# Weight decoding over two queued parts, later global exponentials, and a dense piece moved behind the turns of P

## The chip, the cores and the metric

The kernel runs on one core of one Trainium2 chip. The metric is the device time of one execution in microseconds (us), lower is better. TensorE multiplies matrices into PSUM; VectorE, ScalarE (ACT) and GpSimd (POOL) do elementwise work, each in the order of its own instruction queue; SyncE (SP) issues the DMAs. All of them meet only through semaphores, so a wait on one engine holds whatever stands behind it on that engine.

## The reference

The program computes a local attention with global tokens, then a dense feed-forward layer, then a mixture of experts.

```python
s_g = scale * np.matmul(q_g, k_all.transpose(0, 1, 3, 2))
out_g = np.matmul(sm(s_g), v_all)                    # 32 global queries see all keys
mask = np.abs(pos[:, None] - pos[None, :]) <= 32
s_l = np.concatenate([s_lg, np.where(mask, s_ll, -1e9)], axis=-1)
out_l = np.matmul(sm(s_l), np.concatenate([v_g, v_l], axis=2))
...
h = x @ w_in                                         # 2176 x 512 by 512 x 2048
x = (np.maximum(h, 0) + alpha * np.minimum(h, 0)) @ w_out
...
out[mask_e] = np.maximum(x[mask_e] @ w1[e], 0) @ w2[e]   # 8 experts, assigned greedily
```

There are 4 batches of 8 heads with 512 local and 32 global tokens and a head size of 64. The weights of the first dense layer arrive as float64, as pairs of 32-bit words, and are turned into fp32 on the chip ("decoded").

## The kernel before

The attention runs over 8 groups of four heads (index p), each in 4 steps of 128 queries (index j), so over 32 steps n = 4p + j, with two more to drain. Dense work is woven into it. It is software-pipelined by hand: `attention()` writes out the order of the instructions of TensorE, VectorE and ACT, and that order is kept.

One step n works on three steps' data at once. `norm` (L400) divides the probabilities of step n - 1 by their sums on VectorE. `scores` (L369) multiplies queries and keys of step n on TensorE (L388); four times VectorE adds the mask and takes the maximum (L394) and ACT takes the exponential with its sum (L396); GpSimd adds a small number to the sums (L398). Then `later` holds small VectorE work left over from the step before, among it the copy of the global attention output from PSUM (L472) and the global normalisation `gnorm`. `dense.close` finishes a dense row block: VectorE, ACT and GpSimd make its high and low halves. `wide_part` does the global queries: in a group's second step (j = 1) `gscores`, two matmuls with two VectorE maxima (L438) and one exponential on ACT (L442); in the fourth (j = 3) `gtrans`, which turns the global probabilities by TensorE (L461) in two parts; in the first and third `gpv`, their product with V (L470). `pv` (L421) multiplies the turned probabilities of step n - 2 with V, and `ptrans` (L410) turns those of step n - 1, "the turns of P".

From step BEG = 12 on, `dense.products` adds one piece of six matmuls per step of the first dense chunk, written out right behind the scores. A row block takes two pieces; its ReLU on ACT (L545) opens the next step (`dense.turn`). After the attention `dense.rest` goes on with that chunk, and the later chunks follow, on TensorE in an order written by hand.

`bank` gives PSUM buffers. The pool with the tag "y" has two buffers, which are taken in turn: a step takes one for the output of `pv` and then one for its global work. So the second part of the turn in the fourth step (`gt1`) gets the buffer of the third step's `gpv`, which L472 empties in the fourth step's `later`, behind the four masks of that step. SOLO is 8.

The first halves of the two dense weights are decoded in 16 parts during the attention. `decoding` (L77) is a generator: a DMA load (L79), one magnitude on ACT (L83), four VectorE instructions (L85, L88, L90, L92), and then a conversion on ACT and a subtraction on GpSimd (L72, L73). It yields "A" or "V" for the engine that comes next. `queue` holds two parts; `fill(kind, n)` drives up to n stages of that kind, and before the change only those of the queue's head. There are three load buffers.

SyncE's and GpSimd's orders are not fixed by hand in this stretch.

Of the kernel before, what the change touches and what calls it, by code (L numbers as in the profile page):

```python
# [14 lines left out]
AF = mybir.ActivationFunctionType  # L15
OP = mybir.AluOpType
# [9 lines left out]
def tile_attention_moe_moe(ctx: ExitStack, tc: tile.TileContext, qkw, vw,  # L26
                           w_in, w_out, gate, w1, w2, out):
    nc = tc.nc
    V, A, P, T = nc.vector, nc.scalar, nc.gpsimd, nc.tensor
# [282 lines left out]
    with ExitStack() as at:  # L312
# [11 lines left out]
        SOLO = (S // (4 * WIN)) * (H // 4)  # L324
        BEG = SOLO + 4

        def bank(shape, name):
            pool, tag = pY, "y"
            if name == "s" and wide[0]:
                pool, tag = pS, "s"  # L330
            elif name == "s":
                pool, tag = ((pS, "s"), (pS, "s"), (pH, "h1"), (pH, "h1"))[turn[0] % 4]
                turn[0] += 1
            elif name in ("t", "gs0", "gt0"):
                pool, tag = pX, "x"
            return pool.tile(shape, F32, name=name, tag=tag)
# [4 lines left out]
        G = [dict() for _ in range(NU // 2)]  # L341
# [29 lines left out]
        def scores(p, j):  # L371
            d = G[p]
            if j == 0:
                b, hp = units[2 * p]
                if hp == 0:
                    XB[b] = gx.tile([128, KD, ST], F32, name="xb", bufs=2)
                d["x"] = XB[b][:, hp:hp + 2]
            d["pr", j] = pp.tile([128, 4, KW], F32, name="pr")
            d["sm", j] = pp.tile([128, 4], F32, name="sm")
            d["mx", j] = pp.tile([128, 4], F32, name="mx")  # L380
            s = [bank([128, 2, KW], "s") for _ in range(2)]
            for ii in range(0, 4, 2):
                for e in range(2):
                    i = 4 * j + ii + e
                    for a in range(2):
                        u = 2 * p + a
                        for h, r in heads():
                            T.matmul(s[e][lane(2 * a + h, i), ii // 2], queries(u, i)[r], U[u]["k"][r, kpos(i):kpos(i) + KW],  # L388
                                     start=True, stop=True)
            for ii in range(4):  # L390
                i = 4 * j + ii
                m = mask[:, 0 if i == 0 else 2 if i == NQ - 1 else 1]
                sc = pp.tile([128, KW], F32, name="sc", bufs=4)
                V.tensor_tensor_reduce(out=sc, in0=s[ii % 2][:, ii // 2], in1=m, scale=-D ** -0.5, scalar=BIG,  # L394
                                       op0=OP.add, op1=OP.min, accum_out=d["mx", j][:, ii:ii + 1])
                A.activation(out=d["pr", j][:, ii], in_=sc, func=AF.Exp, bias=d["mx", j][:, ii:ii + 1], scale=-1.0,  # L396
                             accum_out=d["sm", j][:, ii:ii + 1])
            P.tensor_scalar(d["sm", j], d["sm", j], 1e-9, None, op0=OP.add)  # L398

        def norm(p, j):  # L400
            sm = G[p]["sm", j]
            V.reciprocal(sm, sm)
            pr = G[p]["pr", j]
            V.tensor_tensor(pr, pr, sm.unsqueeze(2).to_broadcast([128, 4, KW]), op=OP.mult)  # L404

        def ptrans(p, j):
            d = G[p]
            t = bank([128, 4, 128], "t")
            for ii in range(4):
                T.transpose(t[:, ii], d["pr", j][:, ii], ident)  # L410
            d["t", j] = tp.tile([128, 4, 128], F32, name="pt")
            A.copy(d["t", j], t)
# [14 lines left out]
        def gscores(p, part):  # L427
            d = G[p]
            if part == 0:
                d["s"] = (gp.tile([128, NG], F32, name="gsc"), gp.tile([128, 4], F32, name="gmx", bufs=2))  # L430
            sc, mx = d["s"]
            lo, hi = (0, S) if part == 0 else (S, NG)
            s = bank([128, hi - lo], f"gs{part}")
            for i in range(2):
                k = U[2 * p + i]["k"]
                x = k[:, WIN:2 * WIN] if part else k[:, 2 * WIN:KL - WIN].rearrange("p (m c) -> p m c", c=3 * WIN)[:, :, :2 * WIN]
                T.matmul(s[64 * i:64 * i + 64], U[2 * p + i]["g"], x, start=True, stop=True)
            V.tensor_tensor_reduce(out=sc[:, lo:hi], in0=s, in1=gzero.to_broadcast([128, hi - lo]), scale=-D ** -0.5,  # L438
                                   scalar=mx[:, 0:1] if part else BIG, op0=OP.add, op1=OP.min,
                                   accum_out=mx[:, part:part + 1])  # L440
            if part:
                A.activation(out=sc, in_=sc, func=AF.Exp, bias=mx[:, 1:2], scale=-1.0, accum_out=mx[:, 2:3])  # L442
                P.tensor_scalar(mx[:, 2:3], mx[:, 2:3], 1e-9, None, op0=OP.add)
                later.append(lambda: gnorm(p))

        def gnorm(p):
            sc, mx = G[p]["s"]
            V.reciprocal(mx[:, 3:4], mx[:, 2:3])
            own = gpat[:, 2 * WIN:KL - WIN].rearrange("p (m c) -> p m c", c=3 * WIN)[:, :, :2 * WIN]
            V.tensor_scalar(own, sc[:, :S].rearrange("p (m c) -> p m c", c=2 * WIN), mx[:, 3:4], None, op0=OP.mult)  # L450
            V.tensor_scalar(gpat[:, 4 * WIN:5 * WIN], sc[:, S:], mx[:, 3:4], None, op0=OP.mult)
# [32 lines left out]
        later, at_out = [], [None]  # L484

        def wide_part(n):
            p, j = divmod(n, STEPS)
            last = n == STEPS * NU // 2 + 1
            if j == 1 and not last:
                gscores(p, 0)  # L490
                gscores(p, 1)
            if j == 3:
                gtrans(p, 0)
                gtrans(p, 1)
            if p and (j == 0 or j == 2 or last):
                gpv(p - 1, 1 if last else j // 2)

        def attention():
            N = STEPS * NU // 2
            for n in range(N + 2):  # L500
                p, j = divmod(n, STEPS)
                if n < N and p and 2 * p + 2 < NU:
                    (load_qk, load_v)[j // 2](2 * p + 2 + j % 2)
                if n == SOLO - 1:
                    nc.sync.dma_start(out=ag, in_=gate)
                wide[0] = n >= SOLO
                dense.turn(n)
                if 1 <= n <= N:
                    norm(*divmod(n - 1, STEPS))
                if n < N:  # L510
                    scores(p, j)
                while later:
                    later.pop()()
                dense.close(n)
                fill("V", 2)
                o = None
                if n >= 2:
                    o = bank([128, 2, QS], "o")
                    for _ in range((2, 0, 2, 2)[j] if n < BEG else 0):
                        T.matmul(o[:, 0], ident, ident, start=True, stop=True)  # L520
                dense.products(n)
                wide_part(n)
                fill("V", 2 if n >= SOLO and n % 3 == 0 else 1 if n < SOLO else 0)
                if n >= 2:
                    v, j2 = divmod(n - 2, STEPS)
                    pv(v, j2, o)
                if p and j == 3:
                    gout(p - 1)
                if 1 <= n <= N:
                    ptrans(*divmod(n - 1, STEPS))  # L530
                if n > 2:
                    fill("A", 2)
                yield 0
            for f in later:
                f()
            gout(NU // 2 - 1)

        class dense:
            ps, ys, g, at, over = None, [], None, 0, []
# [66 lines left out]
        queue = []  # L606

        def fill(kind, n):
            if not queue:
                return  # L610
            st, at = queue[0]
            while n and at == kind:
                try:
                    at = next(st)
                    n -= 1
                except StopIteration:
                    queue.pop(0)
                    if ahead_:
                        queue.append(ahead_.pop(0))
                        queue[-1][1] = next(queue[-1][0])  # L620
                    if not queue:
                        return
                    st, at = queue[0]
            queue[0][1] = at

        ahead_ = [[win_steps(dc, 0, i), None] for i in range(2 * KD)] + [[wout_steps(dc, 0, i), None] for i in range(KH)]

# [45 lines left out]
    with tc.tile_pool(name="dc2", bufs=1, side="right") as dc, tc.tile_pool(name="pW", bufs=2, space=PSUM) as pW, \  # L673
# [4 lines left out]
        n = 0  # L678
# [20 lines left out]
    with ExitStack() as mo:  # L699
# [713 lines left out]
        for k in range(E):  # L1413
            n = 0.0
# [101 lines left out]
```

## Time and profile before

| | us |
|---|---|
| median of 3 runs (805.73 to 808.45) | 806.33 |
| profiled execution | 808.91 |
| its span on the core | 807.1 |
| TensorE matmul busy (share of the span) | 778.6 (96%) |
| TensorE weight load | 726.1 (90%) |
| VectorE | 451.8 (56%) |
| ACT | 392.4 (49%) |
| GpSimd | 368.1 (46%) |

Busy time of TensorE is modelled, so a high share is not yet a full engine: single waits must be looked for in its timeline. The shares are means over stages with different limits. The span is the profiled one; the median comes from runs without a profile.

### The profile page before, as it was taken

How to read it: one execution, taken by the hardware profiler on the slowest of the kernel's cores; microseconds unless marked ns; L12 is line 12 of the kernel's file. 1: busy time of each engine (PE TensorE's matmuls, PEld its weight loads, DVE VectorE, ACT ScalarE, POOL GpSimd, SP SyncE). 2: the span in 40 equal slices, each digit the busy share in tenths (PEclk: the TensorE clock that was granted, in tenths of full speed). 3: DMA queues.
4: the chain of work that ended last, by engine and by line, in shares of the span. 5: the costliest groups of instructions: out<-in, count | busy, mean ns of one | idle time of the engine just before them, and what ended most of it. 6: DMA issues, size and time to landing. Idle time of an engine off the chain costs nothing.

```text
span 807.1 us, 20873 instructions
## 1 busy us (share of the span) xinstructions
PE 778.6 (96%) x8290; PEld 726.1 (90%) x8290; DVE 451.8 (56%) x1555; ACT 392.4 (49%) x983; POOL 368.1 (46%) x348
## 2 busy tenths in 40 slices
PE   7899899999999999999999999999999999999996
PEld 4777678999999989999999999999899999999994
DVE  5899899265455621433433467776776777651210
ACT  5787788344544443333333425342564554454430
POOL 2243333054443552100000838473798988698611
PEclk9999999999999999999999999999999999999999
DMA  8988783632343112013221236243467656467510
GB/s 342 400 302 292 271 329 128 211 111 95 109 134 108 56 36 79 28 56 95 74 62 51 84 110 228 79 143 94 130 214 209 189 183 196 153 190 207 193 46 28
DMA packets 53850, 121.98 MB, mean 151 GB/s; under 512 B 4600, under 2 KB 26040, under 8 KB 51705
## 3 DMA queue, kind: packets, MB, share of 16 engines
q1 hardware_dynamic: 50825, 111.73, 42.0%
q0 software_dynamic: 2928, 8.92, 3.0%
q8 instruction: 65, 1.06, 0.5%
q14 instruction: 32, 0.26, 0.1%
HBM read 102.80 MB, written 17.83 MB: 149 GB/s over the span
## 4 chain that ended last, share of the span: by engine, by line
PE 72%; DVE 10%; DMA 6%; issue 4%; POOL 4%; ACT 3%; SPq 0%; POOLq 0%; DVEq 0%; ACTq 0%
PE h L200 21%; PE h L1272 10%; PE y L239 9%; PE h L1116 8%; PE h L1136 8%; POOL m L73 2%; DMA raw<-in_moe_w_dram 2%; DVE sc L394 2%; PE o L421 2%; DMA raw<-in_moe_w_in_dram 2%; DVE pr L404 2%; PE h L1349 2%; PE lp L282 2%; PE s L388 1%; PE t L410 1%
## 5 line engine op out<-in xcount | busy, mean ns | idle before, releaser
L73 POOL TENSOR_TENSOR m<-raw,m 128x1024 fp32r<-128x1024 f32 x64 | 152.1, 2399 | 18.5 <-ACT m L72 15.9
L200 PE MATMUL h<-xh,win 128*128 128x272 f32 x704 | 138.6, 291 | 1.4 <-ACT xd L245 1.4
L73 POOL TENSOR_TENSOR gr<-gb,gr 128x272 fp32r<-128x272 f32 x64 | 48.1, 791 | 149.3 <-ACT gr L72 148.9
L200 PEld LDWEIGHTS h<-xh,win 128*128 128x128 f32 x704 | 111.9, 188 | 4.0 <-issue 2.2
L1116 PE MATMUL h<-xsh,m 128*128 128x272 f32 x512 | 103.3, 294 | 0.0
L200 PE MATMUL h<-xl,win 128*128 128x272 f32 x352 | 101.3, 288 | 0.0
L1272 PE MATMUL h<-gr,wout 128*128 128x272 f32 x672 | 95.1, 294 | 0.0
L1136 PE MATMUL h<-hh,m 128*128 128x272 f32 x448 | 92.7, 298 | 0.0
L1272 PEld LDWEIGHTS h<-gr,wout 128*128 128x128 f32 x672 | 87.0, 189 | 0.4 <-ACT gr L72 0.4
L239 PE MATMUL y<-ghi,wout 128*128 128x272 f32 x448 | 86.9, 290 | 0.0
L73 POOL TENSOR_TENSOR glo<-g,ghi 128x272 fp32r<-128x272 f32 x64 | 54.6, 859 | 67.2 <-ACT ghi L72 55.8
L72 ACT CAST m<-raw 128x1024 fp32r<-128x1024 f32 x64 | 65.9, 1049 | 35.7 <-DMA raw<-in_moe_w_dram 35.7
L1116 PEld LDWEIGHTS h<-xsh,m 128*128 128x128 f32 x512 | 81.7, 188 | 0.1
L205 ACT ACTIVATE neg<-h 128x272 f32<-128x272 f32 x120 | 47.6, 397 | 69.3 <-PE h L200 68.6
L1116 PE MATMUL h<-xsl,m 128*128 128x272 f32 x256 | 73.9, 292 | 0.0
L206 DVE SCALAR_TENSOR_TENSOR g<-neg,al,h 128x272 f32<-128x272 f32 x56 | 27.4, 495 | 82.8 <-ACT neg L205 71.5
L1136 PEld LDWEIGHTS h<-hh,m 128*128 128x128 f32 x448 | 72.6, 192 | 0.9 <-issue 0.9
L239 PEld LDWEIGHTS y<-ghi,wout 128*128 128x128 f32 x448 | 70.9, 188 | 0.8 <-issue 0.8
L1136 PE MATMUL h<-hl,m 128*128 128x272 f32 x224 | 66.6, 297 | 0.0
L200 PEld LDWEIGHTS h<-xl,win 128*128 128x128 f32 x352 | 66.3, 188 | 0.0
L239 PE MATMUL y<-glo,wout 128*128 128x272 f32 x224 | 64.6, 288 | 1.1 <-POOL glo L73 1.1
L206 DVE SCALAR_TENSOR_TENSOR gb<-neg,al,h 128x272 f32<-128x272 f32 x64 | 31.3, 496 | 58.7 <-ACT neg L205 58.7
(286 smaller groups left out, 1638.0 us busy)
## 6 DMA issues: line engine op xcount, KB each, us to landing
raw<-in_moe_w_dram SPq DMA_DIRECT2D x64, 512.0 KB, 3.7
vv<-in_v_dram SPq DMA_DIRECT2D x16, 1024.0 KB, 7.3
qk<-in_qk_dram SPq DMA_DIRECT2D x14, 720.0 KB, 8.6
raw<-in_moe_w_in_dram SPq DMA_DIRECT2D x16, 512.0 KB, 5.9
raw<-in_moe_w_out_dram SPq DMA_DIRECT2D x16, 512.0 KB, 4.3
xb<-xs SPq DMA_DIRECT2D x15, 544.0 KB, 3.9
xs<-xb SPq DMA_DIRECT2D x16, 272.0 KB, 5.9
xpart<-xd SPq DMA_DIRECT2D x32, 136.0 KB, 1.7
```

Of the source, the lines that this page charges most:

```text
L72: a = A.copy(hi, src)
L73: return a, (lo_eng or V).tensor_tensor(lo, src, hi.bitcast(F32), op=OP.subtract)
L200: T.matmul(ps, wi[:, w, k, fs], x[:, k], start=i == 0, stop=i == 3 * KD - 1)
L205: A.activation(out=neg, in_=ps, func=AF.Relu, scale=-1.0)
L206: epi[0] = V.scalar_tensor_tensor(g, neg, al1[:, hf * KH + f:hf * KH + f + 1], ps, op0=OP.mult, op1=OP.add)
L239: T.matmul(ps, wo[:, w, f, ds_], x[:, f], start=f == 0 and i == 0, stop=f == KH - 1 and i == 2)
L282: T.matmul(lp[r:r + 32], w, x, start=n < 4, stop=n >= LT - 4)
L394: V.tensor_tensor_reduce(out=sc, in0=s[ii % 2][:, ii // 2], in1=m, scale=-D ** -0.5, scalar=BIG, op0=OP.add, op1=OP.min, accum_out=d["mx", ...
L404: V.tensor_tensor(pr, pr, sm.unsqueeze(2).to_broadcast([128, 4, KW]), op=OP.mult)
L1116: T.matmul(ps, d["w1"][:, w, kk, f * 128:(f + 1) * 128], x[:, kk], start=kk == 0 and i == 0, stop=kk == KD - 1 and i == 2)
L1136: T.matmul(ps, d["w2"][:, w, f, ms], x[:, f], start=i == 0, stop=i == 3 * K3 - 1)
L1272: T.matmul(ps[j], wo[:, w, f, ds_], x, start=f == 0 and a == 0, stop=f == KH - 1 and a == 2)
```

## The change

Three things are changed. First, `fill` looks at both entries of the queue, not only at the head. For "V" it takes the first entry that waits for VectorE and begins anew after each stage; for "A" it goes once over the entries from the last to the first and drives each that waits for ACT by one stage. The amounts change as well: one `fill("V", ...)` of 2 stages, or 3 in odd steps from SOLO on, stands before the global work; the second `fill("V", ...)` behind it (1 stage before SOLO, 2 in every third step after it) goes. Second, the global exponential with its small GpSimd addition leaves `gscores` and becomes `gexp`, called in j = 1 at the end of the step, ahead of `fill("A", 2)`. Third, `dense.products(n)` moves from behind the scores to behind `ptrans`.

```diff
             V.tensor_tensor_reduce(out=sc[:, lo:hi], ...)
-            if part:
-                A.activation(out=sc, in_=sc, func=AF.Exp, bias=mx[:, 1:2], scale=-1.0, accum_out=mx[:, 2:3])
-                P.tensor_scalar(mx[:, 2:3], mx[:, 2:3], 1e-9, None, op0=OP.add)
-                later.append(lambda: gnorm(p))
+
+        def gexp(p):
+            sc, mx = G[p]["s"]
+            A.activation(out=sc, in_=sc, func=AF.Exp, bias=mx[:, 1:2], scale=-1.0, accum_out=mx[:, 2:3])
+            P.tensor_scalar(mx[:, 2:3], mx[:, 2:3], 1e-9, None, op0=OP.add)
+            later.append(lambda: gnorm(p))
...
                 dense.close(n)
-                fill("V", 2)
+                fill("V", 2 + (n >= SOLO and n % 2))
                 o = None
                 if n >= 2:
                     o = bank([128, 2, QS], "o")
...
-                dense.products(n)
                 wide_part(n)
-                fill("V", 2 if n >= SOLO and n % 3 == 0 else 1 if n < SOLO else 0)
                 if n >= 2:
                     v, j2 = divmod(n - 2, STEPS)
                     pv(v, j2, o)
...
                 if 1 <= n <= N:
                     ptrans(*divmod(n - 1, STEPS))
+                dense.products(n)
+                if n < N and j == 1:
+                    gexp(p)
                 if n > 2:
                     fill("A", 2)
...
         def fill(kind, n):
-            if not queue:
-                return
-            st, at = queue[0]
-            while n and at == kind:
-                try:
-                    at = next(st)
-                    n -= 1
-                except StopIteration:
-                    queue.pop(0)
-                    if ahead_:
-                        queue.append(ahead_.pop(0))
-                        queue[-1][1] = next(queue[-1][0])
-                    if not queue:
-                        return
-                    st, at = queue[0]
-            queue[0][1] = at
+            while n:
+                for e in list(queue)[::-1 if kind == "A" else 1]:
+                    if n and e[1] == kind:
+                        n -= 1
+                        try:
+                            e[1] = next(e[0])
+                        except StopIteration:
+                            queue.remove(e)
+                            if ahead_:
+                                queue.append(ahead_.pop(0))
+                                queue[-1][1] = next(queue[-1][0])
+                        if kind == "V":
+                            break
+                else:
+                    return
```

## Rows read from the trace of the kernel before

**Rows 1.** Stages: window; busy us (count) per engine; PEclk, DMA share, GB/s.

```profile
53.11:148.71 95.60, 90.24 (x1920) 73.79 (x1919) 81.55 (x310) 75.34 (x260) 33.45 (x47) 0.98 0.68 247
148.71:500.00 351.29, 348.76 (x2916) 337.01 (x2913) 159.31 (x370) 143.56 (x332) 111.31 (x128) 1.00 0.30 96
```

**Rows 2.** TensorE's timeline, first matmul of `rest`: start, duration, line, [wait].

```profile
148.71 0.40 PE L590 MATMUL y<-ghi,wout 128*128 128x272 f32 x1
```

**Rows 3.** TensorE's timeline, a fourth step's end and the following first step.

```profile
105.47 0.82 PE L461 MATMUL gt<-ident,gpat 128*128 128x128 f32 x6
106.89 1.12 PE L421 MATMUL o<-pt,vv 128*64 128x32 f32 x32 [0.61 <-DVE xb L472]
107.95 0.66 PE L410 MATMUL t<-ident,pr 128*128 128x128 f32 x4
108.53 0.67 PE L388 MATMUL s<-qk 64*32 64x128 f32 x32
109.13 0.39 PE L582 MATMUL h<-xh,win 128*128 128x272 f32 x1
...
110.09 1.01 PE L470 MATMUL go<-gt,vv 128*64 128x32 f32 x24
111.03 1.13 PE L421 MATMUL o<-pt,vv 128*64 128x32 f32 x32
```

**Rows 4.** VectorE's timeline: first mask of second steps, copy L472 of fourth steps.

```profile
58.71 0.28 DVE L394 CUSTOM_DVE_ANT_0 sc<-s,mask 128x128 f32<-128x128 f32 x1
...
68.28 0.18 DVE L472 COPY xb<-go 128x32 f32<-128x32 f32 x1
...
75.73 0.28 DVE L394 CUSTOM_DVE_ANT_0 sc<-s,mask 128x128 f32<-128x128 f32 x1
...
87.30 0.19 DVE L472 COPY xb<-go 128x32 f32<-128x32 f32 x1
...
96.28 0.29 DVE L394 CUSTOM_DVE_ANT_0 sc<-s,mask 128x128 f32<-128x128 f32 x1 [0.64 <-PE s L388]
...
106.57 0.18 DVE L472 COPY xb<-go 128x32 f32<-128x32 f32 x1
...
114.53 0.28 DVE L394 CUSTOM_DVE_ANT_0 sc<-s,mask 128x128 f32<-128x128 f32 x1
...
123.88 0.18 DVE L472 COPY xb<-go 128x32 f32<-128x32 f32 x1
...
131.60 0.28 DVE L394 CUSTOM_DVE_ANT_0 sc<-s,mask 128x128 f32<-128x128 f32 x1
...
140.65 0.18 DVE L472 COPY xb<-go 128x32 f32<-128x32 f32 x1
```

**Rows 5.** TensorE's timeline, the fourth step with the longest wait (step 19).

```profile
87.63 1.77 PE L421 MATMUL o<-pt,vv 128*64 128x32 f32 x32 [2.69 <-DVE xb L472]
```

**Rows 6.** VectorE's groups, 53 to 150 us: busy us, mean ns of one, idle before.

```profile
L404 DVE TENSOR_TENSOR pr<-pr,sm 128x512 f32<-128x512 f32 x21 | 18.4, 874 | 0.7
...
L92 DVE SCALAR_TENSOR_TENSOR mag<-raw,mag 128x512 int32<-128x512 int32 x12 | 8.7, 729 | 0.4
L90 DVE SCALAR_TENSOR_TENSOR mag<-raw,mag 128x512 int32<-128x512 int32 x12 | 8.2, 684 | 0.1
...
L85 DVE TENSOR_SCALAR mag<-mag 128x512 f32<-128x512 f32 x12 | 6.2, 521 | 0.0
L88 DVE TENSOR_SCALAR mag<-mag 128x512 int32<-128x512 int32 x12 | 5.1, 427 | 0.4
```

**Rows 7.** Waits, 53 to 150 us: us in total, times, longest.

```profile
ACT gsc L442 <- DVE gmx L438: 6.1, 5, 1.4
```

**Rows 8.** Timelines of GpSimd and of VectorE at a second step's end.

```profile
81.31 1.28 POOL L73 TENSOR_TENSOR win<-mag,win 128x512 fp32r<-128x512 f32 x1 [0.96 <-ACT win L72]
...
81.33 1.30 DVE L451 TENSOR_SCALAR gpat<-gsc,gmx 128x32 f32<-128x32 f32 x1
```

**Rows 9.** Stages: the stretch behind the longest wait, with its granted clock (PEclk).

```profile
87.60:91.40 3.80, 3.77 (x69) 3.06 (x69) 2.04 (x5) 2.61 (x10) 0.35 (x2) 0.55 0.93 300
```

## The prediction

> **What bounds the kernel now.** I read first the table by stage. In the attention (53.11 to 148.71 us, the part in which dense pieces are woven in) VectorE is busy 81.55 of 95.60 us and TensorE 90.24; afterwards TensorE is busy 348.76 of 351.29 us [rows 1]. So the change can act on the kernel's time only by moving the end of the attention; what follows is a stream of matmuls that starts when the attention lets it and then hardly waits. The end mark is the first matmul of `rest`, at 148.71 us [rows 2].
>
> Second, TensorE's timeline over a step [rows 3]. From start to start: the product with V 1.06, the turns of P 0.58, the scores 0.60, a dense piece 0.96, the global product with V 0.94; the global turn is six matmuls in 0.82, of which two, its second part, come to about 0.25. A step in which nothing waits is 4.14 us (scores, dense piece, global product, V, turns). The only wait of the excerpt is the one of 0.61 us before the product with V in a cycle's fourth step (j = 3), released by VectorE's copy of the global output (L472). That is where TensorE and VectorE meet: the global turn's second part goes into the PSUM buffer which that copy empties, and the copy stands on VectorE behind the four masks and maxima of the same step. (The trace books the wait on the matmuls behind the turn.)
>
> Third, VectorE's marks once in each cycle of four steps: the first mask of each second step (j = 1), and the copy of each fourth [rows 4]. From mask to copy is 9.57, 11.57, 10.29, 9.35 and 9.05 us; from copy to copy 19.02, 19.27, 17.31 and 16.77, in sum 72.37. The first two of these are the disturbed cycles: steps 18 and 21 have four decode instructions each, and at 87.63 TensorE had waited 2.69 us [rows 5]. This loop, VectorE from mask to copy and then TensorE from the turn to the next mask, is what I put the change into.
>
> **Part 1: decoding over both queued parts.** A part costs VectorE four instructions, mean (729 + 684 + 521 + 427) / 4 = 0.59 us [rows 6], 64 for the 16 parts, before and after. Before, in the order of the queue's head alone, they fall 3, 1, 3, 1 in steps 4 to 7, 2 in each of 8 to 11, and then 4, 2, 2 over and over, until step 29. After, I walked the two queue entries through the new loop: 2 in each of steps 4 to 7, then 2 in even and 3 in odd steps, all used, 60 by step 28, 3 in step 29, 1 in step 30. Through step 12 both have issued 20. No VectorE work is saved; it is moved. Between mask and copy lie the decode instructions of a second and a third step: before 4, 6, 6, 4, 2; after 5, 5, 5, 5, 4. So the stretches become 10.16, 10.98, 9.70, 9.94, 10.23: in sum +1.2 us. The SyncE queue: a part's load still waits for the buffer of the third part before; its first use (the magnitude, on ACT) comes one step later than before in nearly all parts, so I cost it at nothing; if a load came late, ACT would hold up the exponentials behind it, and its weight conversion and GpSimd's subtraction with them.
>
> The first mask of the series (58.71) follows step 12, which loses two decode instructions (4 to 2). So this mask gains between 0 and 1.2 us; I take 0.5, under the middle, since it also waits for its scores and for the normalisation ahead of it. The first copy then lands at 58.21 + 10.16 = 68.37, against 68.28.
>
> **Part 2: the global exponentials at the step's end.** ACT waits 6.1 us in five places for VectorE's two maxima, up to 1.4 each [rows 7]; behind it stand the copies of the attention output and of the turned P. After, the exponentials (same work) stand behind those copies; behind them are the weight conversions, the dense ReLU and the next step's four exponentials. The maxima themselves come 0.59 later, as three decode instructions stand ahead of them and not two. The normalisation that uses them is in the next step on VectorE, behind its masks, and has the time. Bounds: a gain of all 1.4 per cycle, if ACT set the end; a loss of 0.59 per cycle, if the next exponentials are held. TensorE's timeline of the excerpt has no wait for the ACT copies, the nearest row to a price; I take zero.
>
> **Part 3: the dense piece behind the turns of P.** TensorE's instructions are the same, so a cycle's floor is the same. But two distances change. (a) In the fourth step the piece of 0.96 us stood between scores and global turn, and covered VectorE's four masks and the copy, about 1 us. Now the turn follows the scores at once, and TensorE waits for the copy. (b) From the copy on, TensorE must do its dense piece as well before the next scores. The loop after: copy 0.18, turn 0.25, V 1.06, turns of P 0.58, dense 0.96, scores 0.60, global product 0.94, V 1.06, turns 0.58, dense 0.96, scores 0.60, 0.07 to the mask: 7.84 us, of which one piece (0.96) is new. The piece of the second step has only changed its place inside the loop. With the four later stretches of part 1 the cycles are 18.82, 17.54, 17.78 and 18.07, in sum 72.21, against 72.37.
>
> Is VectorE late instead? From the copy's start it has that copy (0.18), three decode instructions (1.77), the copy of the turn (half the columns of a normalisation, so about 0.4) and the normalisation (0.87 [rows 6]), 3.2 us; TensorE brings the next scores 0.18 + 0.25 + 1.06 + 0.58 + 0.96 + 0.60 + 0.07 = 3.7 us after it. So VectorE waits some 0.5 us there, where before it was 0.96 less and no wait, and the loop by TensorE holds.
>
> End: from the last copy (140.65) to `rest` were 8.06 us; now step 31's piece (0.96) lies in between: 9.02.
>
> **Sum.** First copy +0.09, four cycles -0.16, end +0.96: +0.9 us at the end of the attention. Behind it TensorE is saturated, so it is handed on. Against the profiled execution: 808.91 us, its span 807.1, so 1.8 lie around it; it would become 809.8. The median of the runs shown is 806.33, 2.6 below the profiled one; I add the difference to the median: 807.2. A measurement of this kernel can tell about 0.3%, 2.4 us, from no change, so this is none.
>
> A rule of the skill bears on the stretches. At 81.31 GpSimd starts a subtraction of 1.28 us and VectorE's 32-column scaling, started at 81.33, takes 1.30 [rows 8]. The Trainium skill, "SBUF — State Buffer", "Who interferes with whom", says that the two engines share a pair of ports and that the later one blocks until the first is done; the trace agrees. By it, subtractions that land on the masks (PSUM and one SBUF operand) would cost VectorE nothing, and up to 1.3 us a cycle would be won; which VectorE instruction each subtraction will meet the rows don't say, and the stretches stand as measured.
>
> **Rivals.**
> A quiet loop, faster. ACT, freed from its wait, gives earlier exponentials and copies; the decode spread keeps VectorE from ever falling behind; subtractions meet masks. Then the new cycles are as the two quiet ones of before, (17.31 + 16.77) / 2 = 17.04. Four of these are 68.16 instead of 72.21: 807.2 - 4.05 = 803.1. For it: the two costly cycles are those with four decode instructions in a step. Against: the loop has one more piece of 0.96 in it, and decode instructions before the copy go from 2 or 4 to 4 or 5 in the quiet cycles.
>
> Clock falls, slower. The wait of 2.69 us was followed by a granted clock of 0.55 (the 1.2 GHz level; elsewhere 1.00, 2.4 GHz) from 87.6 to 91.4 [rows 9]: the product with V took 1.77 instead of 1.12 [rows 3, 5], and 3.8 us at 0.55 are 1.7 us of work lost, all in the loop. After the wait of 0.61 us the same product took 1.12, so there it did not fall. The new wait in each fourth step is the cycle less four steps of work, 18.0 - 16.4 = 1.6 us, between the two. Should the clock fall in two of five cycles: 807.2 + 3.4 = 810.6; in all five 815.7. It decides from the first or second fall on (0.9 + 1.7 = 2.6). The Trainium skill's "TensorE: Matmul & The Clock Gate", "What's actually happening", has it that the throttled state is the default and activity lifts it, which speaks against longer idle gaps; the 0.55 agrees, and no row here has a gap of this length.
>
> The change does not do what it says: the queue gives no more instructions per step than before, and the wait moves from ACT to TensorE. That is within the forecast's case.
>
> **How the numbers follow.** Forecast (804.7 to 809) 0.5; quiet loop 0.2; clock falls 0.28; the rest of 0.02 is an attention shift that the later stream swallows, also no change. Faster 0.2, same 0.52, slower 0.28. The range leaves out the faster half of the quiet case and three or more clock falls: 803.0 to 811.0.
>
> **What would show it.** In the profile after: a wait of 1 to 2 us on TensorE in each fourth step from step 15 on, released by L472's copy; copies some 18 us apart; VectorE waiting about 0.5 us for scores in each first step; ACT's wait for the maxima much smaller; `rest` between 148 and 151 us; 64 decode instructions ending a step later. Wrong it is if the fourth step shows no wait (then the quiet loop), or if the granted clock is under 1.00 in several cycles.

## The result: slower, and where the time went

| | before | changed |
|---|---|---|
| median of 15 runs on one chip, us | 808.11 (805.5 to 811.64) | 812.68 (807.93 to 815.8) |
| ratio, 95% interval | 1 | 1.0057 [1.004, 1.0073] |
| profiled execution, its span, us | 808.91, 807.1 | 815.08, 813.3 |
| granted TensorE clock, mean of that span | 0.994 | 0.989 |
| first matmul of `rest`, us | 148.71 | 152.29 |

The forecast was 807.2 us and no change; the changed kernel is 0.6% slower. (In its code L472, the copy, is L474; the scalings L450 and L451 are L452 and L453, the turn L461 is L463, the global exponential L442 is L444, `rest`'s L590 is L593.)

The end mark first, and TensorE's waits in the fourth steps on the way to it. TensorE's timeline of the changed kernel: start, duration, line, [wait and its releaser].

```profile
51.81 0.69 PE L463 MATMUL gt<-ident,gpat 128*128 128x128 f32 x2 [2.05 <-DVE xb L474]
52.43 1.93 PE L421 MATMUL o<-pt,vv 128*64 128x32 f32 x32
...
72.93 1.12 PE L421 MATMUL o<-pt,vv 128*64 128x32 f32 x32 [1.24 <-DVE xb L474]
...
79.32 0.66 PE L410 MATMUL t<-ident,pr 128*128 128x128 f32 x4 [1.33 <-DVE sm L402]
...
91.98 1.12 PE L421 MATMUL o<-pt,vv 128*64 128x32 f32 x32 [1.64 <-DVE xb L474]
...
127.25 1.12 PE L421 MATMUL o<-pt,vv 128*64 128x32 f32 x32 [1.64 <-DVE xb L474]
...
143.81 1.13 PE L421 MATMUL o<-pt,vv 128*64 128x32 f32 x32 [0.42 <-DVE xb L474]
...
152.29 0.39 PE L593 MATMUL y<-ghi,wout 128*128 128x272 f32 x1
...
190.09 0.39 PE L200 MATMUL h<-xh,win 128*128 128x272 f32 x1 [2.06 <-ACT xd L245]
```

In the fourth steps 15 to 27 the waits are the predicted ones of 1 to 2 us (one more of 1.35 at 109.6), against 0.61 and once 2.69 before [rows 3, 5]; the last one, in step 31, is 0.42. Behind them the product with V keeps its 1.12. Two rows are other things. The wait of 1.33 us is in a first step (16), where the turns of P wait for VectorE. And the wait of 2.05 us is in step 11, before the first moved piece (step 12), and behind it the product with V takes 1.93.

The stages (window; busy us and count of PE, PEld, DVE, ACT, POOL; PEclk, DMA share, GB/s) show why:

```profile
0.00:52.40 52.40, 42.78 (x882) 31.57 (x882) 38.50 (x164) 37.42 (x132) 13.55 (x38) 0.99 0.92 348
52.40:61.00 8.60, 8.60 (x131) 7.60 (x131) 6.26 (x17) 4.83 (x17) 3.68 (x4) 0.50 0.79 309
61.00:152.29 91.29, 83.02 (x1826) 69.71 (x1825) 75.97 (x295) 72.46 (x247) 31.10 (x44) 1.00 0.64 231
152.29:186.00 33.71, 33.47 (x266) 33.03 (x263) 17.74 (x26) 14.54 (x32) 11.54 (x12) 1.00 0.56 179
...
190.00:198.00 8.00, 7.91 (x50) 7.91 (x51) 3.76 (x8) 4.21 (x12) 3.20 (x4) 0.79 0.11 37
198.00:500.00 302.00, 300.88 (x2527) 289.89 (x2526) 132.30 (x319) 121.29 (x280) 91.37 (x106) 1.00 0.27 83
```

For 8.6 us behind that wait the granted clock is 0.50, the 1.2 GHz level; TensorE is busy all that time, at half its clock. A second fall follows the wait of 2.06 us at 190 (8 us at 0.79, so 1.7 us of work; before, that wait was 1.41 and the clock stayed at 1.00). The rest of the attention runs at 1.00.

VectorE's timeline of the changed kernel: the copies of the fourth steps, and ahead of the first one two long instructions.

```profile
46.67 1.19 DVE L452 TENSOR_SCALAR gpat<-gsc,gmx 128x512 f32<-128x512 f32 x1
...
49.18 1.63 DVE L404 TENSOR_TENSOR pr<-pr,sm 128x512 f32<-128x512 f32 x1
...
51.58 0.18 DVE L474 COPY xb<-go 128x32 f32<-128x32 f32 x1
...
72.60 0.18 DVE L474 COPY xb<-go 128x32 f32<-128x32 f32 x1
...
91.66 0.18 DVE L474 COPY xb<-go 128x32 f32<-128x32 f32 x1
...
109.28 0.18 DVE L474 COPY xb<-go 128x32 f32<-128x32 f32 x1
...
126.93 0.18 DVE L474 COPY xb<-go 128x32 f32<-128x32 f32 x1
...
143.48 0.19 DVE L474 COPY xb<-go 128x32 f32<-128x32 f32 x1
```

With the copies of before [rows 4] and that of step 11 (50.86 before) the 3.58 us by which `rest` is late split up as follows.

| stretch | before | changed | difference |
|---|---|---|---|
| copy of step 11 | 50.86 | 51.58 | +0.72 |
| copy of step 11 to that of step 15 | 17.42 | 21.02 | +3.60 |
| four cycles | 72.37 | 70.88 | -1.49 |
| last copy to `rest` | 8.06 | 8.81 | +0.75 |
| sum | | | +3.58 |

The cycles that I put the change into became shorter; but before they hold the fall of [rows 9], 1.7 us of work, without which they would be about as long (70.7). All of the loss and more is in the one stretch with the clock at 0.50. Behind `rest` another 0.65 us of wait and 1.7 us of clock at 190 come to 2.4, so 5.9 of the span's 6.2 us are placed.

Why TensorE waits 2.05 us in step 11. The copy is 0.72 us later because a GpSimd subtraction lies under the normalisation (L404), which takes 1.63 us. GpSimd's timeline shows it, and an earlier one under the scaling (L452). That earlier one costs nothing against before: there the two scalings of this step took 0.49 and 1.29 us, here 1.19 and 0.23.

```profile
46.29 1.28 POOL L73 TENSOR_TENSOR win<-mag,win 128x512 fp32r<-128x512 f32 x1 [0.21 <-ACT win L72]
...
48.45 1.81 POOL L73 TENSOR_TENSOR xl<-xb,xh 128x544 fp32r<-128x544 f32 x1
```

In the kernel before, the normalisation began 0.05 us ahead of that subtraction and took 0.69 us. VectorE's timeline there, then GpSimd's:

```profile
49.41 0.69 DVE L404 TENSOR_TENSOR pr<-pr,sm 128x512 f32<-128x512 f32 x1
...
50.86 0.19 DVE L472 COPY xb<-go 128x32 f32<-128x32 f32 x1
```

```profile
49.46 1.85 POOL L73 TENSOR_TENSOR xl<-xb,xh 128x544 fp32r<-128x544 f32 x1 [0.30 <-ACT xh L72]
```

And TensorE arrives 1.09 us earlier: at 49.76, the start of its wait, against 50.85, and without a wait of 0.68 for ACT that stood ahead of the turn. TensorE's timeline of the kernel before, the same step:

```profile
49.70 0.71 PE L520 MATMUL o<-ident 128*128 128x128 f32 x4 [0.68 <-ACT xb L423]
...
51.10 0.44 PE L461 MATMUL gt<-ident,gpat 128*128 128x128 f32 x2 [0.25 <-DVE xb L472]
```

0.72 + 1.09 is the 1.8 us between a wait of 0.25 and one of 2.05. The changed kernel's normalisation ends 0.55 us behind the subtraction that it met (50.81 and 50.26), about its undisturbed length. The Trainium skill, "SBUF — State Buffer", "Who interferes with whom", has a VectorE instruction with both inputs in SBUF contend with GpSimd's reads; 1.63 us against 0.69 agrees.

### The profile page after: what moved, and what is told of

Same layout as the page of the kernel before. It is cut to its first block, busy times and chain, and to the rows that moved or that the text cites. A ratio compares the mean times of both kernels' runs of the same rounds, so it can differ in the third digit from the quotient of the medians.

```text
span 813.3 us, 20855 instructions
## 1 busy us (share of the span) xinstructions
PE 779.6 (96%) x8290; PEld 728.9 (90%) x8290; DVE 452.4 (56%) x1555; ACT 395.2 (49%) x983; POOL 370.3 (46%) x348
## 4 chain that ended last, share of the span: by engine, by line
PE 70%; DVE 8%; DMA 6%; issue 5%; POOL 5%; ACT 4%; SPq 0%; POOLq 0%; DVEq 0%; ACTq 0%
PE h L200 21%; PE h L1274 10%; PE y L239 9%; PE h L1138 7%; PE h L1118 7%; DMA raw<-in_moe_w_dram 3%; POOL m L73 3%; PE o L421 3%; DVE sc L394 2%; PE t L410 2%; DMA raw<-in_moe_w_in_dram 2%; PE h L1351 2%; PE lp L282 2%; PE s L388 1%; DVE pr L404 1%
## 5 line engine op out<-in xcount | busy, mean ns | idle before, releaser
L205 ACT ACTIVATE neg<-h 128x272 f32<-128x272 f32 x120 | 47.6, 398 | 70.7 <-PE h L200 68.5
```

The source lines that it names most:

```text
L205: A.activation(out=neg, in_=ps, func=AF.Relu, scale=-1.0)
```

## Experiments

Two theories are told apart. **Clock**: a wait on TensorE is followed by a stretch at the lower clock, and that is what costs. **Loop**: the moved work itself makes the loop longer, or VectorE does, and the clock matters little. Every kernel ran five rounds (11 or 12 runs) beside the kernel before on the same chip; ratios are to that. The mean granted clock is the median over a kernel's runs.

### One part at a time

e1_dense, the piece alone:

```diff
-                dense.products(n)
                 wide_part(n)
...
                     ptrans(*divmod(n - 1, STEPS))
+                dense.products(n)
```

> The kernel before with only the dense piece moved behind the turns of P. Theory clock (the loss is TensorE's granted clock falling behind a long wait in a fourth step; the loop itself costs nothing): the wait of the turn in step 11 stays as before (0.25 us), since up to step 12 nothing differs; from step 15 on waits of 1 to 3 us in fourth steps, with four decode instructions in steps 18 and 27 the longest; 808 to 812 us by how many of them the clock falls behind. Theory loop (the moved piece lengthens the loop by 0.96 us a cycle, whatever the clock): 808.1 + 5 = 813 us with a granted clock as before.

Measured: 811.01 us, 1.0039 [1.0021, 1.0058], clock 0.994, `rest` at 152.09. Its TensorE timeline and stages have two falls, both in the loop:

```profile
74.71 0.21 PE L421 MATMUL o<-pt,vv 128*64 128x32 f32 x1 [1.52 <-issue]
90.29 1.12 PE L421 MATMUL o<-pt,vv 128*64 128x32 f32 x32 [3.09 <-DVE xb L472]
```

```profile
72.00:80.00 8.00, 6.33 (x107) 4.94 (x107) 4.48 (x20) 4.29 (x19) 1.57 (x3) 0.79 0.62 240
...
88.00:96.00 8.00, 5.71 (x108) 4.98 (x109) 5.42 (x26) 5.21 (x18) 1.49 (x2) 0.79 0.94 348
```

The piece alone loses measurably, inside the range of the clock theory and 2 us under the loop theory's 813. The wait in step 19 is 3.09 instead of 2.69 [rows 5], with the old decode order and its four instructions in step 18. The other fall follows a gap of 1.52 us in which TensorE waited for nothing that the profile shows ("issue").

e2_fill, the decode order and amounts alone: the hunks of `fill` and of its calls. e3_gexp, the later exponential alone: `gexp` cut out of `gscores` and called ahead of `fill("A", 2)`. e4_fill_gexp, both, which is the change without the moved piece.

> The kernel before with only the decoding changed (both queued parts, the new amounts). Theory clock: as in the changed kernel TensorE waits about 2 us for the turn in step 11, as step 9 has three decode instructions and VectorE is late; the clock falls there: 809 to 812 us. Without the moved piece the later cycles have no long waits. Theory loop: no piece moved, so no slower than 808.1 us; rather 805 to 807, as the four-instruction steps are gone.

> The kernel before with only the global exponential moved to the step's end. Both theories: within 0.3% of 808.1 us. If the row normalisation of step 10 now meets GpSimd's subtraction (1.6 us in place of 0.7), theory clock expects the wait in step 11 and the fall here already: 810 to 812 us.

> The changed kernel with the dense piece left behind the scores. Theory clock: step 11 is as in the changed kernel (wait 2.05 us, granted clock 0.50 for 8 us), so nearly all of the loss is still there: 810 to 813 us. Theory loop: 804 to 807 us, the loss is gone with the moved piece.

Measured: e2 809.19 us, 1.002 [1.0002, 1.0037], clock 0.9965; e3 809.84, 1.0019 [0.9995, 1.0043], clock 0.993; e4 807.96, 1.0008 [0.9983, 1.0033], clock 0.994. The profile of each waits in step 11 (1.66, 1.52 and 2.07 us), and the clock falls behind it (0.50 to 0.57 over the next 4 to 8 us); `rest` comes at 150.51, 150.71 and 150.14. So either part by itself opens the wait that I had left unchanged. Two results go against the clock theory. It put e4 at 810 to 813 us, and e4 is not measurably slower than before although its profile has the wait and the fall of step 11; its four cycles (copies at 72.25 and 142.09) take 69.84 us against 72.37. And e2 is slower by 0.002 at a median clock no lower than that of before (0.996). TensorE's timeline and stages of e4:

```profile
52.05 0.69 PE L463 MATMUL gt<-ident,gpat 128*128 128x128 f32 x2 [2.07 <-DVE xb L474]
```

```profile
52.00:56.00 4.00, 3.95 (x54) 3.22 (x62) 3.38 (x6) 2.65 (x10) 1.78 (x2) 0.50 1.00 413
```

In e3 there is also a counterexample, a longer wait with no fall behind it:

```profile
90.75 1.12 PE L421 MATMUL o<-pt,vv 128*64 128x32 f32 x32 [2.41 <-DVE xb L474]
```

```profile
52.00:60.00 8.00, 8.00 (x120) 6.65 (x122) 6.81 (x17) 5.57 (x20) 3.63 (x4) 0.57 0.91 372
...
90.00:98.00 8.00, 6.24 (x150) 5.15 (x153) 6.71 (x25) 6.90 (x26) 2.59 (x5) 1.00 0.97 339
```

### The wait covered, or filled

e5_fourth_back: the changed kernel, but the fourth step's piece stays ahead of the global turn.

```diff
+                if j == 3:
+                    dense.products(n)
                 wide_part(n)
...
-                dense.products(n)
+                if j != 3:
+                    dense.products(n)
```

> The changed kernel, but in every fourth step (j = 3) the dense piece stays between scores and global turn; in the other three it stands behind the turns of P. Theory loop (the moved piece of the fourth step is what is paid for: it no longer covers VectorE's masks and copy, and lengthens the way to the next scores): waits in the fourth steps from 15 on shrink by about 1 us each, rest starts near 149 us plus what step 11 costs, 808 to 809.5 us, mean granted clock up to 0.994. If the place in the other steps matters: 811 to 813 us.

Measured: 808.32 us, 0.9997 [0.9977, 1.0018], clock 0.992, `rest` at 148.08, 0.63 earlier than before. In its profile step 11 waits 1.97 us without a fall; the only fall of its attention is at 32 to 36, ahead of step 11. The loss is gone when the one piece that covered the masks and the copy stays where it was; pieces of other steps may move. The time is where the loop theory put it (808 to 809.5). The clock is only 0.002 above the changed kernel's, so what e5 takes away is not all clock.

e6_warm: the changed kernel, with four matmuls in the wait, between the two parts of the turn, in fourth steps from step 11 on. They write into a buffer that the next product overwrites; nothing of the computation changes. The four calls are eight matmuls in the trace (L497 below).

```diff
                 gtrans(p, 0)
+                for _ in range(4 if n >= 11 else 0):
+                    T.matmul(o[:, 0], ident, ident, start=True, stop=True)
                 gtrans(p, 1)
```

(`wide_part` gets `o` as an argument for it.)

> The changed kernel with four extra 128x128 matmuls with the identity (1.3 us) between the two parts of the global turn in the fourth steps from step 11 on; their results are overwritten. They fill the wait with work. Theory clock: behind steps 11 and 15 to 31 the granted clock stays at 1.00, mean granted clock 0.996 or more, time 808 to 809.5 us, though work is added. Theory loop alone: 812 to 813 us, and slower where the wait is under 1.3 us.

Measured: 806.93 us, 0.9989 [0.9971, 1.0007]; clock 0.998, in no run under 0.996, where the changed kernel's median is 0.990. TensorE's timeline and stages of e6:

```profile
49.94 1.06 PE L497 MATMUL o<-ident 128*128 128x128 f32 x8
52.16 0.44 PE L463 MATMUL gt<-ident,gpat 128*128 128x128 f32 x2 [1.16 <-DVE xb L474]
...
149.09 0.39 PE L595 MATMUL y<-ghi,wout 128*128 128x272 f32 x1
```

```profile
52.40:61.00 8.60, 8.33 (x207) 6.68 (x206) 8.35 (x29) 8.03 (x29) 4.82 (x5) 1.00 0.94 364
61.00:149.09 88.09, 83.89 (x1797) 71.36 (x1793) 74.53 (x285) 69.59 (x236) 29.98 (x43) 1.00 0.64 235
```

This is the plainest comparison of the study. The copy of step 11 is no earlier than in the changed kernel (51.92; there 51.58), so TensorE is released as late; but part of its wait is filled, 1.16 us of it are left, its clock stays at 1.00, and in the 8.6 us in which the changed kernel ran 131 matmuls it runs 207. From that copy to the next are 17.41 us, against 21.02 in the changed kernel and 17.42 before. The cycles are 17.94, 17.88, 17.91 and 16.82.

e7_fill_gexp_warm: the same four matmuls in e4. e8_before_warm: in the kernel before.

> Decoding and global exponential as changed, the dense piece behind the scores as before, and the same four extra matmuls. Theory clock: the fall behind step 11 (8 us at 0.50 to 0.70) is gone, 804.5 to 806.5 us, faster than the kernel before. Theory loop: the waits in its later fourth steps are 0.9 to 1.25 us, so the extra matmuls cost 0 to 0.4 us a cycle: 808 to 809.5 us.

> The kernel before with the same four extra matmuls. Theory clock: the fall at 87.6 us is gone (1.7 us), but its waits in the fourth steps are 0.2 to 0.7 us but for step 19, so the extra matmuls cost up to 1 us in each of four cycles: 807 to 810 us with mean granted clock 0.997 or more.

Measured: e7 807.87 us, 0.9984 [0.9966, 1.0001], clock 0.997; e8 810.43, 1.0011 [0.999, 1.0033], clock 0.995. e7 and e6 differ by the moved piece alone, at the same clock, and their intervals lie on each other: with the wait partly filled the moved piece costs nothing that can be measured (to some 1.5 us). Three cautions. In e8 the matmuls gain nothing; time and clock miss what was expected (807 to 810 us, 0.997), and its profile fell twice (behind waits of 1.73 us in the loop and 2.92 us at the later wait for ACT). e7 misses the 804.5 to 806.5 us of the clock theory and is no faster than e4 (807.96); its profile has a fall at 40 to 44 us (0.57), ahead of step 11, with no wait above 0.99 us before it. And e5 and e7 are, like e6, no measurable gain on the kernel before.

### Which wait, and where the matmuls stand

e9_dense_warm: e6's four matmuls in e1. e10_warm_11: the changed kernel with seven in step 11 alone. e11_warm_15: with four, from step 15 on. e12_fourth_back_warm: e5 with seven in step 11 and two later. Only the count differs from e6's edit:

```diff
+                for _ in range(4 if n >= 11 else 0):                         # e9
+                for _ in range(7 if n == 11 else 0):                         # e10
+                for _ in range(4 if n >= 15 else 0):                         # e11
+                for _ in range(7 if n == 11 else 2 if n >= 15 else 0):       # e12
```

> The kernel before with only the dense piece moved, and four extra matmuls in the fourth steps from step 11 on. Theory clock (the moved piece costs only by clock falls behind the waits it opens): mean granted clock 0.996 or more, 807 to 808.5 us, 3 less than without the extra matmuls (811.0). Theory loop (0.96 us a cycle, whatever the clock): 810 to 811 us at a clock of 0.996 or more.

> The changed kernel with seven extra matmuls (2.3 us) in step 11 alone. If the fall behind step 11's wait is the larger part of the loss: median granted clock 0.994 or more, 808 to 809.5 us. If it is the waits of 1.2 to 1.6 us in the five later fourth steps: clock 0.991 or 0.992, 811 to 812 us.

> The changed kernel with four extra matmuls in the fourth steps from step 15 on, none in step 11. The counterpart: if step 11 is the larger part, 810 to 812 us with a clock of 0.991 to 0.993; if the later waits, 808 to 809 us with 0.995 or more.

> A version meant to beat both: the changed kernel, the dense piece of the fourth steps left behind the scores, seven extra matmuls in step 11 and two in each later fourth step. Theory clock: granted clock 0.997 or more; rest begins at 147.5 to 148.5 us as the waits are shorter; 804 to 806 us. If short waits cost nothing and the clock falls by chance anyway: 807 to 808.5 us, as without the extra matmuls (808.3).

Measured: e9 810.55 us, 1.0034 [1.0019, 1.0049], clock 0.995. e10 810.74, 1.0026 [1.001, 1.0042], 0.996. e11 810.33, 1.0032 [1.0006, 1.0058], 0.9945. e12 807.85, 0.9992 [0.9976, 1.0009], 0.996. Filling step 11 alone (e10), or all fourth steps but 11 (e11), leaves the kernel measurably slower than before; filling all does not (e6). So no one of the waits is the whole. e12 came where its second reading had it, not at 804 to 806 us. Two results don't fit the clock theory. e10 is slower by 0.0026 at a clock of 0.996, the median of before, and lies in neither of its two ranges. The other is e9. The piece moved by itself stays slower with the filling, and its clock went up only from 0.994 to 0.995; its step 19 still waits 2.26 us beside the four matmuls, with no fall behind that in the profile. Part of the piece's cost with the old decode order may be loop and not clock. e10's profile fell at 76 to 84, behind an "issue" gap of 1.96 us.

e13_warm_7_4: the changed kernel with seven in step 11 and four in each later fourth step. e14_after_wait: e6's four, but behind the second part of the turn, and so behind the wait. e15_changed_again: the changed kernel once more.

```diff
                 gtrans(p, 0)
+                for _ in range(7 if n == 11 else 4 if n > 11 else 0):        # e13: ahead of the wait
+                    T.matmul(o[:, 0], ident, ident, start=True, stop=True)
                 gtrans(p, 1)
+                for _ in range(4 if n >= 11 else 0):                         # e14: behind it
+                    T.matmul(o[:, 0], ident, ident, start=True, stop=True)
```

> The changed kernel with seven extra matmuls in the wait of step 11 and four in those of the later fourth steps. Theory clock: median granted clock 0.997 or more, 806 to 807.5 us, 4 to 6 us under the changed kernel on the same chip. If step 11 and the later waits had been measured right as 2 us each and nothing else: 808 to 809 us.

> The changed kernel with four extra matmuls in each fourth step from step 11 on, but behind the wait (after the second part of the turn). Theory clock: the wait stays empty, the granted clock stays near 0.990, and 1.3 us of work is added in six places: 815 to 821 us. If the extra matmuls help in another way than by filling the wait: under 812 us.

> The changed kernel once more, as the reference for the two others on this chip: 811.5 to 813.5 us with a median granted clock of 0.989 to 0.992.

Measured: e13 809.76 us, 1.0001 [0.9983, 1.0018], clock 0.9965. e14 814.0, 1.006 [1.0039, 1.0082], 0.9955. e15 812.08, 1.0038 [1.0013, 1.0062], 0.990. In the wait such matmuls gain 2.3 us against e15 (e13, with three more calls in step 11; 4 to 6 us were expected), behind it they lose 1.9. For the time it is their place that counts. Two things don't fit. e14's clock should have stayed at about 0.990 and rose to 0.9955, though its wait is there (1.98 us in step 11, with 0.50 behind it), and its time is 1 us under what was expected. A group of four calls takes 1.08 us there (from its start at 92.75 to the next product at 93.83), so six groups are some 6.5 us of TensorE's time, and the time is up by 1.9. The higher clock would give back 3.0 of that by the fit in the table below; the rest is open. And e13, with seven calls in step 11, is not down to e6's 806.93; the two ratios differ by 0.0012, inside their intervals.

e15's profile repeats the fall behind step 11 and has two more in the loop:

```profile
52.00:63.00 11.00, 11.00 (x170) 9.27 (x172) 6.83 (x18) 7.06 (x23) 3.79 (x5) 0.53 0.77 302
...
76.00:84.00 8.00, 6.42 (x122) 5.11 (x106) 4.68 (x23) 4.73 (x18) 2.31 (x3) 0.79 0.55 212
...
127.00:136.00 9.00, 7.36 (x139) 6.35 (x138) 6.98 (x27) 6.69 (x24) 2.70 (x4) 0.81 0.63 231
```

There the waits are 2.04 us (step 11), 1.57 at 79.7 (inside the window; no larger wait of TensorE precedes that fall) and 1.64 at 129.0, the same length that was followed by no fall in the first profile. `rest` starts at 155.41.

### Clock and time over all runs

| kernel | runs | clock, median | us, median | runs at 0.996 or more: us, median | us per 0.01 of clock (fit) |
|---|---|---|---|---|---|
| before | 134 | 0.996 | 807.87 | 807.36 (68 runs) | 5.4 |
| changed, and e15 | 15 and 12 | 0.990, 0.990 | 812.68, 812.08 | 807.93 (5 runs, 807.32 to 810.36) | 5.7, 5.4 |
| e6_warm | 12 | 0.998 | 806.93 | 806.93 (12 runs) | |

The row "before" holds the runs beside the experiments. The clock differs from run to run of one kernel, and the time goes with it in part (correlation -0.67 in the 134 runs). The changed kernel's median is lower by 0.006, and 0.006 at 5.4 us per 0.01 is 3.2 of the 4.6 us that it loses. The 1.3 us left are of the size of the 0.9 that the loop sum gave. This split is an estimate from the fit, and not shown: e2 and e10 are slower than before at its median clock, and e5 got back 4.4 us with 0.002 of clock, which the fit puts at 1.1. At a high clock (0.996 or more) the medians are: changed 807.9, before 807.4, e4 806.7 (5 runs), e5 805.9 (4 runs), but e2 809.0 (11 runs) and e10 810.1 (7 runs). So e4 and e5 are a microsecond or so quicker at equal clock and give it back in the clock (0.994 and 0.992), and the fourth step's piece, moved and with the wait unfilled, costs one to two. With so few runs that is a reading and not shown.

## Why the prediction was wrong

The forecast of no change fell; the rival "clock falls" came true, given 0.28. In the profile the loss at the end of the attention (3.58 us) is where that rival put it, in a stretch of lower granted clock (+3.60) behind a wait that TensorE did not have before. Over all runs the lower clock goes with some 3.2 of the 4.6 us by the fit; how the median loss divides between clock and loop is not shown.

**The start of the series was the step that failed.** The sentence "Through step 12 both have issued 20" counted decode instructions only in sum, and the forecast let everything ahead of 58.71 stand but for a gain of 0.5 us in the first mask. The first copy came at 72.60, not 68.37: the term "First copy +0.09" of the sum measured +4.32 us, of which 0.72 are the late copy of step 11 and 3.60 the slow stretch behind it. The changed step is not the first one that a change reaches: `fill` and `gexp` were at work long before step 12, and e2, e3 and e4, each without the moved piece, all wait 1.5 to 2.1 us in step 11. Two things make that wait, as the two timelines show: VectorE's copy is late because a subtraction now begins ahead of a normalisation and no longer just behind its start, and TensorE is early because a wait for ACT is gone. I had written that "which VectorE instruction each subtraction will meet the rows don't say", and then let the stretches stand as measured; it should have gone into the range as a late copy. This is the step of the profiled execution; e4 has the same wait and fall and loses nothing measurable, so over many runs it takes the uncovered waits of Part 3 as well.

**The size of a fall was the other.** "1.7 us per fall" came from one fall in the attention of before, 3.8 us at 0.55 [rows 9]. The fall in step 11 is 8.6 us at 0.50, or 4.3 us of work, of which 3.6 reached the next copy. The rival's condition, "from the first or second fall on", held: one such fall (3.6 us) and a smaller one behind `rest` (1.7) are 5.3 of the 6.2 us by which the profile is longer.

**Part 1** was right in its cycles as far as one execution tells: 19.06, 17.62, 17.65 and 16.55 us against 18.82, 17.54, 17.78 and 18.07. The first of them agrees by luck: its stretch from mask (81.36) to copy is 10.30, not 10.98, and the way from copy to mask 8.76, not 7.84, with the wait of 1.33 in step 16 that no term had. The 64 decode instructions end in step 30 (the last at 140.91), before in step 29. Only the last cycle was missed: its stretch from mask (134.44) to copy is 9.04 us, not 10.23. Its two added decode instructions found room, since the wait of 0.49 for the sums and a scaling of 1.29 us under a subtraction, both in that stretch before, are gone (0.23 now).

**Part 2**, the exponentials at zero: by itself the change is not measurable in time (e3), so the price held as far as that tells, but it opened the wait in step 11 and, in its profile, the fall behind it. That ACT's wait would be much smaller came true; the row of waits of the changed kernel, over 53 to 155 us, against [rows 7] (us in total, times, longest):

```profile
DVE sc L394 <- PE s L388: 7.0, 7, 2.5
...
ACT gsc L444 <- DVE gmx L438: 1.9, 5, 0.6
```

6.1 us of ACT's waiting became 1.9, and nothing was won by it. The first row is VectorE waiting for scores, in the cycles' first steps 0.19 to 0.72 us each, about the 0.5 forecast; the longest, 2.5, is at 62.7 and belongs to the slow clock.

**Part 3**: the waits of 1 to 2 us in the fourth steps are there, the end is +0.75 (forecast +0.96), and in the three changed kernels with added matmuls whose profiles have no fall in the attention (e6, e11, e13) `rest` comes at 149.09, 149.83 and 150.00, about where the sum put it (148.71 + 0.9). So the loop sum was sound to half a microsecond there, and the quiet loop at 803 was not reached. But taking the cover from the wait was the decisive edit in time: the piece alone loses 0.0039, all but the piece 0.0008, and the change with only the fourth step's piece left back is at 0.9997.

**The weighing.** I took waits of 0.61 and 2.69 us in one trace as the ends between which 1.6 lies, and called no fall the likelier. But the same trace has two waits of TensorE between those ends, behind `rest`, and a second fall. TensorE's waits from 150 to 807 us (us in total, times, longest) and a stage of the kernel before:

```profile
PE pq L1011 <- DVE m L1001: 1.8, 1, 1.8
PE h L200 <- ACT xd L245: 1.4, 1, 1.4
```

```profile
620.00:630.00 10.00, 8.24 (x63) 7.90 (x60) 6.63 (x31) 4.41 (x8) 7.78 (x4) 0.86 0.52 165
```

Behind the 1.4 us, at 185, the clock stayed at 1.00; behind the 1.8 us, at 626.6, it is 0.57 from 627 to 631. So "elsewhere 1.00" did not hold, and the nearest wait above 1.6 us with a fall behind it was 1.8, not 2.69. I asked of each wait whether the clock falls, and not how often in many executions. The profile shows one execution; in e15 the same code fell three times in its attention.

**What stays open.** The length of a wait does not decide a fall. In the attention of these profiles the clock fell behind waits of 1.52 (e3), 1.64 (e15), 1.66, 1.73, 1.98, 2.04, 2.05, 2.07, 2.69 and 3.09 us, and not behind 1.64 (changed, twice), 1.75 (e10), 1.97 (e5), 2.06 (e11), 2.26 (e9) and 2.41 (e3). The Trainium skill, "TensorE: Matmul & The Clock Gate", "What's actually happening", has the throttle follow how busy TensorE has been lately; that would leave room for both, but no run here shows what it goes by. Open too are what e2, e9 and e10 lose, why e14's clock rose, and the 1.3 us at equal clock. No version was measurably faster than the kernel before.

## What to carry to other kernels

Where TensorE stands close to saturated, an uncovered wait can cost more than its own length again, in the granted clock of the microseconds behind it (here 4.3 us of work behind 2.05 us). So look at what covers a known wait before moving it, keep an independent piece (or matmuls whose output is overwritten) in the wait and not behind it, and read the clock per stage beside every wait. A change's price starts at the first step its code reaches, not at the step that it was made for; and where an outcome hangs on the clock, judge by the mean clock of many runs, not by the stage of one profile.

## What the runs showed of the hardware

- One wait of 2.05 us was followed by 8.6 us at a granted clock of 0.50, four times the wait.
- Falls also follow gaps in which TensorE waited for nothing that the profile shows: "issue" gaps of 1.52 us (e1), 1.96 us (e10) and, the smallest, 0.90 us (e5). But the kernel before has the same gap of 0.90 at 31.08 us with no fall behind it. TensorE's timeline and stages of e5:

```profile
31.78 0.65 PE L421 MATMUL o<-pt,vv 128*64 128x32 f32 x14 [0.90 <-issue]
...
53.53 0.44 PE L463 MATMUL gt<-ident,gpat 128*128 128x128 f32 x2 [1.97 <-DVE xb L474]
```

```profile
32.00:36.00 4.00, 4.00 (x58) 3.24 (x55) 2.84 (x14) 2.78 (x10) 0.08 (x1) 0.57 0.97 354
36.00:148.08 112.08, 103.28 (x2304) 85.91 (x2302) 99.27 (x372) 90.30 (x312) 40.94 (x56) 1.00 0.71 260
```

- The spread between runs of one kernel goes in part with its mean granted clock, about 5.4 us per 0.01 over 134 runs of the kernel before (correlation -0.67).
